# A four-layer attention kernel whose step order, engine choices and buffer assignment are replaced as a whole

## The chip, the cores and the metric

The kernel runs on one core of a Trainium2 chip. The core has five engines that each work through a queue of their own in order: TensorE (PE, matmuls into the eight banks of PSUM), VectorE (DVE), ScalarE (ACT), GpSimd (POOL) and SyncE (SP, which here does nothing but issue DMA transfers). Engines wait for each other through semaphores. The metric is the device time in microseconds from the start of the program to its end, as the median of several runs.

## The reference

A sequence of 2048 rows of 512 values in bf16 goes through four layers: A, B, A, B. Each layer normalises its input, computes attention with 32 heads of 16 values, multiplies with an output matrix and adds the result to its input. Both A layers share one set of weights, both B layers another.

```python
def _A_ref(x, wqkv, w_phi, wo):                    # H = 32, Dh = 16
    ...
    pq = jnp.einsum("bhsd,hdf->bhsf", q, w_phi)
    pk = jnp.einsum("bhsd,hdf->bhsf", k, w_phi)
    phi_q = jnp.concatenate([_softmax(pq, axis=-1), _softmax(-pq, axis=-1)], axis=-1)
    phi_k = jnp.concatenate([_softmax(pk, axis=-1), _softmax(-pk, axis=-1)], axis=-1)
    kv = jnp.einsum("bhsf,bhsd->bhfd", phi_k, v)
    z  = jnp.einsum("bhsf->bhf", phi_k)
    ...
    o = num / den                                   # num = phi_q kv, den = phi_q z + 1e-6
    return o_reshaped @ wo

def _B_ref(x, wqkv, wo):
    W, dil = 8, 2
    ...
    idx = pos[:, None] - off[None, :]               # each row sees itself and 7 rows before, 2 apart
    ...
    attn = _softmax(logits, axis=-1)
    o = jnp.einsum("bhsw,bhswd->bhsd", attn, vg)
    return o_reshaped @ wo

x = x + _A_ref(_layernorm(x), A_wqkv, A_w_phi, A_wo)
x = x + _B_ref(_layernorm(x), B_wqkv, B_wo)
x = x + _A_ref(_layernorm(x), A_wqkv, A_w_phi, A_wo)
x = x + _B_ref(_layernorm(x), B_wqkv, B_wo)
```

## The kernel before

**Tiles.** The 2048 rows are cut into four blocks of 512 columns, called block 0 to 3 below. `x` stays in SBUF from the first layer to the last. Within a block most tiles are 128 x 512: `xn` (normalised `x`), `xnT` (its transpose, on PE through `ident` at L478 to L490, or by a DMA at L473), `K`, `QT`, `V`, `oT` (the attention's result, transposed).

**Layer A.** For each block, `a1` makes the feature maps of the keys: PE multiplies (L616), ACT takes the exponential (`Ek`, L622), DVE sums and divides (L649 to L674), PE multiplies the values (L628) and adds up the key-value sums (L691). The values are copied to `vaug` by ACT or DVE. `a2` does the same for the queries (L721, `Eq` L729), and PE sums each softmax with 32 small matmuls (`ms`, L737). Once the sums over all four blocks are there, `akv` copies them to `kvT`, PE transposes them (L767) and DVE writes them into `ZM` (L776) and `R` (L780). Then come the denominators (`a3`, L805 to L872) and the output (`a4`, L924, L543).

**Layer B, general form.** `b1` makes `K`, `QT` and `V` of a block (L951). K and V carry a few columns of the block before (the halo). SP copies V eight times into `Vg`, once for each place in the window (L1012). `b2`: DVE multiplies `QT` with shifted `K` (`prod`, L1043, 128 x 4096 values in one instruction), PE adds the products up per head through `indQK` (L1050), ACT takes the exponential, and the softmax ends with `PT` (L1078) on DVE. `b3`: DVE multiplies `PT` with `Vg` (`pav`, L1105, 128 x 4096 values), PE adds up through `indAV` (`mo`, L1114, 32 x 32 matmuls with `pav` as the weights), the result is copied to `oT`, and four matmuls with `WoB` (L543) make the output of 128 rows. There are four `pav` and four `mo` per block.

**The last block.** Block 3 of the second B layer has a form of its own (`e1` to `e4`): scores as small matmuls (`sc`, L1278), the exponential `ex` (L1299), a mask on DVE (`msk`, L1304), `mo` as 64 tiny matmuls (L1322), the division by the sums (`ln`, `rd`, L1338 and L1341) as DVE's `oB` (L1349), PE's transposes to `oT`. It goes in four parts `t` = 0 to 3.

**The residual.** For each 128 rows a `res` step adds the layer's output to `x`. It has two forms: DVE adds from PSUM (L556), or PE adds `x` in PSUM through a matmul with `ident` (L546) and ACT copies the sum out (L553). ACT's squares `sqd` (L563) and a few small operations then give the mean and the deviation for the next layer's `xn` (L466 on DVE or L468 on ACT). In the last layer `x` goes to the output (L567) instead.

**What sets the order.** Nothing is scheduled by rule. All work is recorded as 1488 small steps, each a few instructions that belong together, in named threads (`step`, L188). `run` (L1450) plays them in the order that the string `_ORDER` gives, one name in base 36 after the other. Since every engine works in order, this string fixes the queue of every engine, of PE, DVE, ACT, POOL and of SP's DMA issues. A `flex` step (L196) may run on two engines; the string `_CHOICE` holds a bit for each. For copies and `xn`, 1 is DVE and 0 is ACT; for `res`, 1 is the form with PE and ACT; for `bev`, 1 lets DVE read PSUM with no copy by ACT.

**Buffers.** Each tile asks `slot` (L161) for the next entry of `_SLOTS` of its kind: `med` (16 buffers), `ps` (eight PSUM banks), `big` (eight buffers of 128 x 4096, for `prod`, `pav`, `Vg` and others) and `t2` (six). A tile waits for the tile that had its buffer before. So the strings also fix who waits for whom.

**The flag.** The fast form is right only where some sums stay in bounds. The `flag` steps count this: two on DVE, one on PE. Then every engine loads the flag from memory (`flag`, L1411) and branches (`If`, L2069): where the flag is set, `_general_path` computes all again. With this input it isn't set. `_OPT["flag_lag"]` is 12: the load is issued as the twelfth step counted from the last DVE flag step, on SP between the stores of the output.

Of the kernel before, what the change touches and what calls it, by code (L numbers as in the profile page):

```python
# [52 lines left out]
    "flag_lag": 12,  # L53
# [8 lines left out]
8 2e a d c 23 i i i 0 j 9 k j l i 2 i i i i 0 b o p i f 2 0 1m 1m 1o m n i i i i 1n 1m 1m 1p 1q 1m 1r o q r 1m t  # L62
4 z 1s s z i 3 1t 1u 21 z z 10 3 1t i7 1v 22 22 21 1 24 24 2p z 0 t u 13 11 15 1t 1t t 16 1w 1t 1y 12 12 12 12
1x x 1t 5 v w w 25 y 14 2f 2f 18 18 18 18 1z 2g 2c 17 6 19 18 1c 1d 39 2d 1b 1a 2d 22 22 1f 1f g 21 22 22 3a 3a
2c 2c 1f 2d 20 21 1f 22 2c 7 7 20 20 22 26 29 1g 1f 1k 39 3a 2d 2d 2d 2d 1i h 3b 2f 24 2i 1h 1e 29 1j 1l 2q 2h
27 2d 2n 3c 2o 2o 29 29 2a 39 2k 2k 3a 2k 2k 2n 2n 2n 2q 2o 2o 2r 3a 3a 2q 2q 2o 2o 2o 29 2y 2y 2l 2s 2k 2o 2z
2z 2z 2z 31 31 36 3c 33 24 36 36 28 36 2y 2y 2v 2v 2z 2v 37 36 2z 2z 2z 2f 2j 2u 2v 2b 2w 2b 2b 2b 2m 36 2m 36
2m 36 36 2m 39 3a 3b 3b 31 2v 2t 3a 31 32 4e 37 3c 34 35 39 3a 2x 2x 3c 2x 30 2x 38 38 36 38 38 3i 3c 3b 3c 3c
3c 7 3d 3e 3e 3j 3k 3k 3b 3k 3c 3l 5h 3m 3n 3m 3d 3e 3d 3l 5i 3o 3m 3e 3e 3l 3p 3m 3q 3r 3m 3m 5j 3d 3v 5i 3e 3e
3s 3e 20 20 20 20 3t 3m 5h 3u 5n 3m 3m 5m 3d 3e 7c 5h 5q 5o 5p 5r 5k 5i 3f 3g 3g 7 3f 3g 3g 5l 3m 5i 5i 7d 3w 3x  # L70
5i 5i 3z 5i 5i 3f 3f 7e 5i 5s 3g 3y 3g 40 41 7d 5w 42 7f 41 41 7f 41 5t 7f 3g 5v 3g 5u 5x 44 43 45 bd 43 43 46
43 47 5y 3f 43 47 48 90 5x 5x 4b e 49 4c 60 61 41 41 4a 41 41 3g 5x 5z 5z 4d 4g 4g 4h 5z 62 5z 4l 4l 4l 91 92 7d
7d 7g 63 4i 5z 91 4f 4n 4q 4q 4m 4q 63 66 67 64 65 7j 7i 7h 4l 7k 4r 93 4g 4g 4j 4w 4w 7l 7l 4o 4w 7o 68 4k 4q
4u 93 93 4t 4s 4f 7l 7p 7m 7n 4p 4v 7n 7l 7q 6p 6k 6k 4v 6k 7n 7n 91 91 6f 6g 7r 6n 6m 6k 6a 6a 4w 94 6l 7n 69
7r 7u 6o 7v 96 7t 97 4x 95 7s 7w 98 4x 4x 4x 6f 6c 6h 4y 4y 6a 6d 6b 6r 6r 99 6f 6i 6r 99 3h 99 99 9d 9e 3h 6f
6j 6a 6e 9a 9b 9c 9b 6r 9b 9b 83 7y 7y 84 9f 9b 8d 7z 6s 6s 6s 9f 9h 6s 6t 6t 88 89 9i 7y 6s 6t 4w 4x 83 83 6q
6q 7y 6q 85 88 4y 88 8b 83 9g 87 86 81 b2 9j 9k 88 8c 9m 9n 8f 9w 9x 82 9w 9w a1 6r 9z 69 6u 9w 80 6u 6v 8a 6u
6v 6x 6v 4w 6w 6q 6u 6v 6y 9m 4v 4z 4z 6z 4v 70 71 4z 4z 70 70 9y 72 7x 73 72 74 70 75 72 72 76 9o 9r 9r 50 51
8f 50 50 72 52 76 78 8e 8e 50 53 77 54 9r 9u 79 7a 9m 9p 7b 8f 9s 9t 55 8e 56 57 8f 55 58 55 55 59 8g 8g 8g 8e
a0 8g 57 57 a3 9r 5a 57 9v 9m 9q 5b a3 57 5b 8h 8h 5c b3 5e 5d 5f 5g 7x 9l a2 b0 b0 a3 b1 b1 b1 8g 8h b1 b3 b3  # L80
b6 b3 b7 bz c0 c0 a4 a4 a4 a3 a4 a5 a5 bz c0 c0 bz d3 b4 bz c0 c0 c0 c0 8f 8i b0 b1 a4 8i 8i 8i a5 as at b0 b1
# [12 lines left out]
ex ey ey f8 fa dm dm dm dm ew f0 fa f6 f2 hu hv f5 es ga dn dn hw f1 dk i1 i2 i1 dl dm f9 f9 i3 c6 i6 i6 i6 hx
hw hw dn hy fb i6 fa fb fa fb hz fb fc hu gl fc fb c5 fc gl dl do gn gl c6 dp do dp i1 i1 fa i6 i6 gb i8 i4 i9
gc i9 i5 ib go ia i6 f9 f9 i9 i9 i6 do ie id gb i6 i6 i6 dr gm gg gh hw i0 gd gg gi ic ic dp ds dq do dp dt ic
fd fe fd fe fd fg fe i6 i6 i6 i6 fh i6 c5 gb ge ic ff ic gg gj if ic ic if ic ic ic if ig ig gq gg gb gl gk gf
ig gs gs gs if if ig ig gp du if ig gs gt gt gt gt if gu ig if du du gu du dv ic c5 ic ic fd ih fe ih ih dy ig
ih ic dz ic dw ii ii fi ij gr gr gt ij ik ij ij fj fj ik il ga gu il in gs fl ii ij ij gv ii fj fj im ij ij ik
il ik fn fo gr gr il gw gx iq io iq iq gv gw gv gw gv gv ip iq iv dx dx fk fm fm gy gz h2 is gw gw ir it h2 iw  # L100
iu h0 it ix iw h3 h3 h4 h5 h6 h2 h1 h3 h7 h2 h5 h3 h8 h5 h5
# [4 lines left out]
    "0010110111100111111111000000100000100110011100000111011110010100000101010000100000000000111101011100"  # L106
    "1010010100001100100000000000000011111110000100001010100000000000000000010111001000001101000000000000"
    "1010000011111100000000000100010110011011010100101111000000001001000000010110010001000100011100100000"
    "00000000011111010000011100000000000000000000000001000011001000000000000000001100"
)  # L110


_SLOTS = {
    "med": (
        "0123456789abcdef346aff72ffc3105f92b4de6a7fd92b317ef99962c0517dbf2e3abf6925cd13e273a31dad901d74235cdb"
        "f72a94d35c017b9264acf31d08"
    ),
    "ps": (
        "0123124350123021456715604156734153267234701623047237452365001230210345672135304675261473045672350146"
        "1401230453013042567103651251741023452036714302310345031240230435406703203501467012012457245201240310"  # L120
        "3245602750235102563740130473024567142362047540123640760437034563745101021345067241301456701236204531"
        "7024560124567326452016435735601247351204561203460750264012312301203405367136731421432102324567467556"
# [15 lines left out]
class _Fast:  # L138
# [1311 lines left out]
    def run(self):  # L1450
        self.setup()
        self.stages()
        n, left = {}, None
# [647 lines left out]
```

## Time and profile before

| | us |
|---|---|
| median of 3 runs | 329.32 |
| the three runs | 329.32, 327.63, 330.07 |
| span of the profiled execution | 327.7 |
| DVE `pav` L1105, 29 instructions | 63.3, one 2.219 |
| DVE `prod` L1043, 28 instructions | 62.9, one 2.285 |
| PE projections of B L951, 336 matmuls | 76.7, one 0.380 |
| ACT exponentials L622 and L729, 64 each | 33.9 and 34.7 |

The time of the profiled execution is its span, 327.7 us, 1.6 below the median. The page lists each engine's busy time over that span; PEld are PE's weight loads, which run beside its matmuls. In rows of groups, `A<-B` means that the instruction writes tile A from tile B, `x45` counts instructions, and the numbers behind the bar are the busy time of all, the mean ns of one, and the idle time of the engine just ahead of them, with the tile that ended the wait. In rows of the timeline the first number is when the group starts in the span, the second how long it lasts, and a bracket holds the idle time ahead of it. In rows of stretches come the stretch, its length, the busy time of PE, PEld, DVE, ACT and POOL (each with its count of instructions), the share of full speed at which PE's clock was granted, the busy share of the DMA engines and the GB/s.

The layers follow each other and overlap: the last `mo` of the first A (L924) starts at 98.2 us, when the first projections of B (from 77.3 us) are long under way; the last `mo` of the first B (L1114) starts at 177.3, the first keys of the second A (L616) at 148.0; the second A's last `mo` starts at 242.1 us, and the tiny matmuls of the last block (L1322) run from 298.3 to 308.9.

### The profile page before, as it was taken

The page shows a single profiled execution, that of the slowest core. Times are in us where ns is not written, and L with a number is a line of the kernel's source. Part 1 is how long each engine was busy: PE and PEld are TensorE (multiplying, and loading weights), DVE is VectorE, ACT ScalarE, POOL GpSimd, SP SyncE. Part 2 cuts the span into 40 slices and gives each one's busy share as a digit, 9 for nine tenths or more (in the row PEclk, how much of TensorE's full clock was granted, in tenths as well). Part 3 has the DMA queues.
Part 4 walks back from the last instruction along what each step waited for, and adds up shares of the span by engine and source line. Part 5 has one row for each costly group of instructions (what it writes and reads, how often), then busy time and mean ns, then how long its engine had stood idle before and what let it go on. Part 6 is the DMA issues. An engine that isn't in the chain of part 4 may idle for free.

```text
span 327.7 us, 8877 instructions
## 1 busy us (share of the span) xinstructions
PE 308.8 (94%) x3542; PEld 153.5 (47%) x3574; DVE 296.3 (90%) x456; ACT 278.1 (85%) x640; POOL 39.1 (12%) x64
## 2 busy tenths in 40 slices
PE   7999999899999999999999999789999999986993
PEld 3644456444444454444444455543545444443441
DVE  6899995989999999999999999599898999999493
ACT  4999989999789977999999999799898866987360
POOL 6000000000020006000000000000040395210000
PEclk9999999999999999999999999999999999999799
DMA  7964300023677979679991200050588997549814
GB/s 203 341 162 90 108 2 4 2 68 81 144 172 140 132 149 158 108 131 131 145 121 28 40 0 4 4 141 9 145 147 121 192 136 131 135 83 176 158 67 137
DMA packets 45793, 36.41 MB, mean 111 GB/s; under 512 B 30832, under 2 KB 41136, under 8 KB 45744
## 3 DMA queue, kind: packets, MB, share of 16 engines
q1 hardware_dynamic: 45216, 35.75, 56.2%
q8 instruction: 30, 0.49, 0.7%
q14 instruction: 19, 0.16, 0.2%
q10 hardware_dynamic: 528, 0.02, 0.1%
HBM read 11.13 MB, written 3.25 MB: 44 GB/s over the span
## 4 chain that ended last, share of the span: by engine, by line
DVE 31%; ACT 31%; PE 18%; issue 12%; DMA 3%; SPq 2%; DVEq 0%; ACTq 0%
DVE prod L1043 6%; ACT Eq L729 5%; DVE pav L1105 5%; PE PS L543 5%; ACT sqd L563 5%; ACT Ek L622 4%; DVE x L556 4%; DVE Ek L674 3%; PE PS L951 3%; DVE xn L466 3%; ACT oT L205 2%; PE PS L1050 2%; DVE s L649 2%; ACT xn L468 2%; DMA wraw<-in_A_wqkv_dram 1%
## 5 line engine op out<-in xcount | busy, mean ns | idle before, releaser
L951 PE MATMUL PS<-xnT,WB 128*128 128x512 bf16 x336 | 76.7, 380 | 0.3 <-ACT K L205 0.2
L1105 DVE TENSOR_TENSOR pav<-PT,Vg 128x4096 bf16<-128x4096 bf16 (+1 forms) x29 | 63.3, 2219 | 0.6
L1043 DVE TENSOR_TENSOR prod<-QT,K 128x4096 bf16<-128x4096 bf16 x28 | 62.9, 2285 | 0.4 <-ACT QT L205 0.3
L951 PEld LDWEIGHTS <-WB 128*128 128x128 bf16 x336 | 37.3, 114 | 37.1 <-issue 4.2
L543 PEld LDWEIGHTS <-oT 128*128 128x128 bf16 x240 | 22.5, 98 | 31.3 <-issue 5.6
L729 ACT ACTIVATE Eq<-PS 128x512 bf16<-128x512 f32 x64 | 34.7, 624 | 0.0
L622 ACT ACTIVATE Ek<-PS 128x512 bf16<-128x512 f32 x64 | 33.9, 627 | 0.0
L563 ACT ACTIVATE sqd<-x 128x512 bf16<-128x512 bf16 x48 | 30.4, 633 | 2.1 <-DVE x L556 1.2
L721 PE MATMUL PS<-xnT,WA 128*128 128x512 bf16 x128 | 31.1, 380 | 0.2 <-ACT bs L870 0.2
L543 PE MATMUL PS<-WoB,oT 128*128 128x512 bf16 x105 | 27.7, 393 | 3.1 <-issue 2.9
L616 PE MATMUL PS<-WA,xnT 128*128 128x512 bf16 x124 | 29.9, 379 | 0.5 <-DVE x L556 0.2
L628 PE MATMUL PS<-WA,xnT 128*128 128x512 bf16 x122 | 29.9, 379 | 0.3
L543 PE MATMUL PS<-WoA,oT 128*128 128x512 bf16 x119 | 29.3, 380 | 0.8 <-DVE x L556 0.2
L556 DVE SCALAR_TENSOR_TENSOR x<-PS,x 128x512 bf16<-128x512 f32 x45 | 28.9, 684 | 0.3 <-PE PS L543 0.2
L205 ACT CAST oT<-PS 128x512 bf16<-128x512 f32 (+1 forms) x47 | 24.8, 595 | 3.8 <-PE PS L1114 3.5
L616 PEld LDWEIGHTS <-xnT 128*128 128x128 bf16 x128 | 12.3, 98 | 15.0 <-issue 0.6
L628 PEld LDWEIGHTS <-xnT 128*128 128x128 bf16 x128 | 12.3, 98 | 14.4
L205 ACT CAST V<-PS 128x512 bf16<-128x512 f32 x27 | 15.4, 591 | 4.1 <-PE PS L951 4.1
L674 DVE TENSOR_TENSOR Ek<-Ek,rk 128x4096 bf16<-128x4096 bf16 (+1 forms) x10 | 18.6, 1860 | 0.3 <-ACT rk L669 0.3
L721 PEld LDWEIGHTS <-WA 128*128 128x128 bf16 x128 | 11.7, 97 | 15.2 <-issue 2.0
L205 ACT CAST K<-PS 128x512 bf16<-128x512 f32 x30 | 17.4, 591 | 0.3 <-PE PS L951 0.3
L466 DVE TENSOR_SCALAR xn<-x,rstd,nmr 128x512 bf16<-128x512 bf16 x46 | 16.8, 408 | 0.6
(164 smaller groups left out, 496.9 us busy)
## 6 DMA issues: line engine op xcount, KB each, us to landing
Vg<-V SPq DMA_DIRECT2D x112, 131.5 KB, 4.8
Prho<-rd SPq DMA_DIRECT2D x8, 512.0 KB, 5.4
x<-in_A_x_dram SPq DMA_DIRECT2D x3, 512.0 KB, 5.8
WB<-in_B_wqkv_dram SPq DMA_DIRECT2D x3, 512.0 KB, 8.6
out_dram<-x SPq DMA_DIRECT2D x6, 256.0 KB, 2.3
wraw<-in_A_wqkv_dram SPq DMA_DIRECT2D x4, 256.0 KB, 5.4
vd<-Vs SPq DMA_DIRECT2D x2, 272.0 KB, 3.3
x<-in_A_x_dram SPq DMA_DIRECT2D x4, 128.0 KB, 3.9
```

Source lines behind the costliest of these rows:

```text
L205: self.nc.scalar.copy(out=out, in_=in_)
L543: nc.tensor.matmul(y[:], lhsT=lh(t, c), rhs=Wo()[:, c, :], start=(c == 0), stop=(c == NB - 1 and not onpe))
L556: nc.vector.scalar_tensor_tensor(out=xb[:, t, :], in0=T[t][:], scalar=1.0, in1=xb[:, t, :], op0=ALU.mult, op1=ALU.add, **kw)
L563: nc.scalar.activation(out=sqd[:], in_=xb[:, t, :], func=ACT.Square, accum_out=T["ss"][:, t:t + 1])
L616: nc.tensor.matmul(pk[:], lhsT=xnT[:, t, k, :], rhs=self.WA[:, k, D:2 * D], start=(k == 0), stop=(k == NB - 1))
L622: nc.scalar.activation(out=T["E"][:, t, s, :], in_=T["k", t][:], func=ACT.Exp, scale=1.0 - 2.0 * s)
L628: nc.tensor.matmul(pv[:], lhsT=xnT[:, t, k, :], rhs=self.WA[:, k, 2 * D:3 * D], start=(k == 0), stop=(k == NB - 1))
L721: nc.tensor.matmul(pq[:], lhsT=self.WA[:, k, hb * P:(hb + 1) * P], rhs=xnT[:, :, k, :], start=(k == 0), stop=(k == NB - 1))
L729: nc.scalar.activation(out=self.Eq[L, b][s][:, :, hb, :], in_=T[hb][:].rearrange("p (t i) -> p t i", t=4), func=ACT.Exp, scale=1.0 - 2.0 * s)
L951: nc.tensor.matmul(pp[:], lhsT=self.WB[:, k, i * D + c:(i + 1) * D:NB], rhs=xnT[:, :, k, :], start=(k == 0), stop=(k == NB - 1))
L1043: nc.vector.tensor_tensor(out=pr[:], in0=QT[:, c:c + 1, :].to_broadcast([P, NW, TB]), in1=win, op=ALU.mult)
L1105: nc.vector.tensor_tensor(out=pv, in0=PT[:, :, lo:lo + n].unsqueeze(1).to_broadcast([P, NB, 2, n]), in1=vw, op=ALU.mult)
```

## The change

The diff replaces `_ORDER`, `_CHOICE` and four of the five strings of `_SLOTS`; the fifth, `pp`, stays. None of the functions that issue instructions is changed. The flag's load becomes a step of its own (`read`), placed by `_ORDER` like any other, and here it is the last step of all. `flag_lag` goes.

```diff
-    "flag_lag": 12,
...
 _ORDER = """
-8 2e a d c 23 i i i 0 j 9 k j l i 2 i i i i 0 b o p i f 2 0 1m 1m 1o m n i i i i 1n 1m 1m 1p 1q 1m 1r o q r 1m t
...
-iu h0 it ix iw h3 h3 h4 h5 h6 h2 h1 h3 h7 h2 h5 h3 h8 h5 h5
+ce e4 4f 8 i i i i i i i i i 23 5k ck i i f a 3t 3u d 2 9 0 h e 3r 5o 5l ci e3 3p 0 1m 3o i j o 2 ch k b j l 4
...
+gw h0 gw h2 iv h3 h1 h3 h2 h3 h2 iw iu it it h4 h5 h6 h7 h3 h5 h5 h8 h5 iy
 """
...
 _CHOICE = (
-    "0010110111100111111111000000100000100110011100000111011110010100000101010000100000000000111101011100"
...
+    "1010111111110111111110100000100000011000000000000111011110000100001101010110000000000000110111101100"
...
     "big": (
-        "012345670123456012345617234561720351724361720436170425361725362503421034210354276"
+        "472307531426351062154643273172617351305205426165704562316152365205402314240230610"
...
+        def read():
+            self.redo = self.flag()
+
         add("flag", "DVE", counts)
         add("flag", "PE", total)
         add("flag", "DVE", decide)
+        add("flag", "ALL", read)
...
-        n, left = {}, None
+        n = {}
         for w in _ORDER.split():
             key = self.names[int(w, 36)]
             i = n.get(key, 0)
             n[key] = i + 1
             self.threads[key][i]()
-            if key == "flag.DVE" and i == 1:
-                left = _OPT["flag_lag"]
-            if left is not None:
-                left -= 1
-                if left == 0:
-                    self.redo = self.flag()
-        if left is None or left > 0:
-            self.redo = self.flag()
```

Decoded, the new strings do this to the instructions. The counts of all instructions that run on one engine alone stay the same. Of the steps that may run on two engines, 5 copies of `vaug`, 4 of `oT` and one of half `kvT` go from DVE to ACT; 3 `xn` and one `xnT` go from ACT to DVE; 3 `res` go from PE with ACT to DVE, so that the matmuls with `ident` fall from 19 to 16. At the start, SP issues the half key weights first and the weights of B in one go behind `x`, and eleven instead of nine warm-up matmuls stand ahead of PE's first transposes. At both turns from keys to queries the transposes of `kvT` come earlier in PE's queue: four query matmuls stand ahead of them instead of eight in the first A, and all of a block's `ms` behind them instead of ahead in the second. In the second B, block 0's four `mo` come late and in a row, and block 1's third `pav` takes the buffer that its first `pav` had. In the last block, the first two `mo` stay side by side, and the third and fourth do as well; 18 output matmuls, three `res`, one mask and two `pav` stand between the first two parts' `oB` and the third's. The code above the flag moves up by one line, so that every line number below `flag_lag` is one less in the changed kernel, up to the flag steps.

More of the change, by code (lines that the diff above doesn't have):

```diff
@@ L67 @@
[L67 to L81, printed above, removed]
@@ new lines @@
+3 3 1m m 0 0 i p o 2e 1 q 6 1n 1o z i r 5 1m 1m z n z 1m z s 20 20 20 20 1t 20 1m 1p 1t 1v 1q 1r 1s 21 20 7 21
+1u 10 24 z 22 1t 11 22 13 t 1t 1t 15 12 25 1x 16 12 22 14 24 t 18 e7 22 1t 1w 18 12 12 1z 2c 17 u t v x 2d 2d
+2c 2c 2c 2f 18 2d w 26 w 2d 18 2f 2d 2p 1f 2d y 19 1y 18 1b 1c 1a 1d 2f 1e 2g 20 2d 1f 39 2i 2h 1f 39 3a 7 1f
+21 2d 39 3a 3a 2k 3a 1g 1f 5q 1j 2f 21 7 7 3a 1i 24 24 1h 22 22 c 22 2n 22 2j 1k 2n 3a 27 29 29 1l 2n 2o 2n 2k
+2o 3s 2o 29 29 2o 28 2o 2q 3b 2o 2o 2o 2v 2a 2y 2z 2z 2y 2y 2k 2z 29 2z 2y 2z 2z 31 2k 2r 2l 31 36 2v 2q 36 36
@@ new lines @@
+2q 2z 2z 33 3c 39 36 2b 2b 2k 2v 32 2t 37 2b 2b 2m 2m 2v 3a 2m 3b 36 36 g 2q 3c 2w 31 3a 3c 2s 2v 31 36 36 36
+35 34 39 30 3c 2m 2x 37 2x 2x 2u 3b 3c 36 3a 3b 2x 38 38 38 38 3d 3c 3i 3j 3c 3k 3c 3e 3b 3k 3l 3m 5h 3e 3d 3c
+3n 3e 3e 3d 3k 3m 3l 5i 3e 3m 3l 3m 3q 3m 3d 3e 5j 3m 5i 3v 3e 3e 5h 3m 5i 3d 5m 3m 7c 5i 5n 3m 3e 7d 3m 5h 5i
+5i 5p 5i 5i 5i 5r 3f 3g 3g 3f 3g 3w 3g 3f 3x 3z 5i cd 3y 7e 40 3f 3g 3g 7d 7f 5s 7f 5u 3g 41 5t 3g 41 5v 7f 41
+42 5w 43 44 41 45 43 46 5x 43 43 5y 5x 47 3f 43 90 3g 60 47 48 49 5x 4c 41 4b 91 41 41 41 4d 5x 4a 92 4q 91 93
@@ L110 @@
+    "1000000011111100000000000000100110011011100100111010100011000100000000001110010000010010011010000000"
+    "00000000011010101000011100000000000000000000000000000001000000000000000000001000"
 )
```

73 lines of the change are left out of this document (38 added, 35 removed).

## The prediction

> **What bounds the kernel now.** I read the page's busy times first, then the chain of waits, then the stretches of the span, then groups of instructions for prices, and last the timeline where the change moves something.
>
> ```profile
> PE 308.8 (94%) x3542; PEld 153.5 (47%) x3574; DVE 296.3 (90%) x456; ACT 278.1 (85%) x640; POOL 39.1 (12%) x64
> ...
> DVE 31%; ACT 31%; PE 18%; issue 12%; DMA 3%; SPq 2%; DVEq 0%; ACTq 0%
> ```
> ```profile
> 0.00:53.00 53.00, 50.42 (x555) 27.55 (x561) 46.85 (x102) 45.85 (x97) 6.09 (x35) 1.00 0.52 140
> 53.00:207.00 154.00, 150.71 (x1569) 73.50 (x1581) 145.43 (x205) 144.59 (x336) 10.26 (x16) 1.00 0.54 93
> 207.00:327.70 120.70, 107.70 (x1420) 52.46 (x1432) 104.03 (x149) 87.67 (x210) 22.74 (x13) 0.98 0.63 121
> ```
> ```profile
> 280.00:300.00 20.00, 18.73 (x400) 9.34 (x401) 19.44 (x14) 17.28 (x43) 3.51 (x2) 1.00 0.59 125
> 300.00:310.00 10.00, 7.33 (x175) 3.90 (x176) 5.21 (x6) 4.07 (x13) 0.00 (x0) 0.83 0.97 180
> ```
>
> Three engines are nearly full (columns of the stretches: PE, PEld, DVE, ACT, POOL). From 53 to 207 us each has at most 9.4 us without work, so the chain jumps between them and no single one sets the time. Only after 207 us is there slack: 13.0 us on PE and 16.7 us on DVE, and 4.8 us of DVE's lie between 300 and 310. A new order can win there, or win by doing less work on whichever engine the chain runs through. It has as much room to lose: two or three engines at 94% cover nothing.
>
> The profiled execution took 327.7 us; the median of the runs is 329.32. I make the sum on 327.7 and add 1.6 at the end.
>
> **Term 1: work that changes its engine.** The `_CHOICE` bits move these steps. DVE loses 5 copies of `vaug`, 4 of `oT` and one of half `kvT`, and gains 3 `xn`, one `xnT` of 1024 columns and 3 residual adds `x`. ACT takes and gives the counterparts. PE loses 3 matmuls with `ident` (the residual added in PSUM).
>
> ```profile
> L466 DVE TENSOR_SCALAR xn<-x,rstd,nmr 128x512 bf16<-128x512 bf16 x46 | 16.8, 408 | 0.6
> L556 DVE SCALAR_TENSOR_TENSOR x<-PS,x 128x512 bf16<-128x512 f32 x45 | 28.9, 684 | 0.3 <-PE PS L543 0.2
> L203 DVE CAST oT<-PS 128x512 bf16<-128x512 f32 x14 | 9.4, 682 | 0.0
> L203 DVE CAST vaug<-PS 128x512 bf16<-128x512 f32 x8 | 5.4, 679 | 0.0
> L205 ACT CAST oT<-PS 128x512 bf16<-128x512 f32 (+1 forms) x47 | 24.8, 595 | 3.8 <-PE PS L1114 3.5 <-PE PS L924 0.2
> L205 ACT CAST vaug<-PS 128x512 bf16<-128x512 f32 x24 | 13.4, 604 | 0.0
> L468 ACT ACTIVATE xn<-x,nmr,rstd 128x512 bf16<-128x512 bf16 x18 | 14.3, 814 | 1.7 <-DVE nmr L457 1.7
> L553 ACT ACTIVATE x<-PS 128x512 bf16<-128x512 f32 x19 | 11.2, 598 | 2.0 <-PE PS L546 2.0
> L205 ACT COPY xnT<-PS 128x1024 bf16<-128x1024 bf16 (+1 forms) x6 | 5.3, 891 | 0.0
> L546 PE MATMUL PS<-x,ident 128*128 128x512 bf16 x19 | 7.7, 406 | 0.0
> ```
>
> DVE: 3 x 0.408 + 3 x 0.684 + 0.68 - 5 x 0.679 - 4 x 0.682 - 0.5 = -2.7 us (the `xnT` copy is put at an `oT` cast's 0.68, of as many bytes; the half `kvT` costs at most one, 0.68 on DVE and 0.60 on ACT, and I take 0.5 for it on both). ACT: 4 x 0.595 + 5 x 0.604 + 0.5 - 3 x 0.814 - 3 x 0.598 - 0.89 = +0.8 us. PE: -3 x 0.406 = -1.2 us. Everything else is the same count of the same instructions. Weighted with the engines' shares of the chain: -2.7 x 0.31 + 0.8 x 0.31 - 1.2 x 0.18 = **-0.8 us**. The ends are -2.7 (all of DVE's saving lies on the path) and +0.8 (ACT's extra lies on it and nothing is won).
>
> **Term 2: the two turns from keys to queries.** When the last sums of `kvT` are done, PE transposes it and DVE makes `ZM` from it; both wait in a row.
>
> ```profile
> 52.01 1.90 PE L721 MATMUL PS<-xnT,WA 128*128 128x512 bf16 x8
> 52.12 0.69 DVE L203 CAST kvT<-PS 128x512 bf16<-128x512 f32 x1 [0.96 <-PE PS L691]
> 53.75 0.39 PE L767 MATMUL PS<-ident,kvT 128*128 128x128 bf16 x4
> ...
> 54.27 0.29 DVE L776 TENSOR_TENSOR ZM<-PS,maskH 128x32 bf16<-128x32 bf16 x2 [1.46 <-PE PS L767]
> ```
> ```profile
> 206.53 0.58 ACT L205 CAST kvT<-PS 128x512 bf16<-128x512 f32 x1
> 207.19 0.52 PE L737 MATMUL PS<-Eq,indS 128*32 128x128 bf16 x24 [0.48 <-ACT kvT L205]
> 207.64 0.40 PE L767 MATMUL PS<-ident,kvT 128*128 128x128 bf16 x4
> ...
> 208.15 0.29 DVE L776 TENSOR_TENSOR ZM<-PS,maskH 128x32 bf16<-128x32 bf16 x2 [2.15 <-ACT rS L743]
> ```
>
> In the first turn `kvT` is ready at 52.81 and PE comes to it at 53.75, because eight query matmuls stand ahead; after the change four do, so up to 0.9 us goes. In the second it is ready at 207.11 and the transposes start at 207.64, behind 24 of the 32 small matmuls of `ms`; the change puts `ms` behind them: up to 0.5 us. What is late next is the same in both: the denominators' chain between ACT and DVE. I take half of it, **-0.7 us** (0 to -1.4), since the PE work put behind the transposes delays the next softmax sums.
>
> **Term 3: the last 30 us.** Here DVE carries the end, with one large hole.
>
> ```profile
> 298.45 0.83 DVE L1304 TENSOR_TENSOR et<-et,maskW 128x1280 bf16<-128x1280 bf16 x1 [0.22 <-ACT et L1299]
> ...
> 300.39 1.28 DVE L1349 TENSOR_TENSOR oB<-PS,rdB 128x512 bf16<-128x512 f32 x2
> ...
> 302.03 0.69 DVE L1078 TENSOR_TENSOR PT<-E,rden 128x1024 bf16<-128x1024 bf16 x1 [0.35 <-ACT rden L1073]
> 302.62 1.43 PE L543 MATMUL PS<-WoB,oT 128*128 128x512 bf16 x4 [2.55 <-issue]
> ...
> 304.27 1.91 PE L543 MATMUL PS<-WoB,oT 128*128 128x512 bf16 x4
> ...
> 309.45 0.69 DVE L1349 TENSOR_TENSOR oB<-PS,rdB 128x512 bf16<-128x512 f32 x1 [4.41 <-ACT rdB L1341]
> ...
> 310.10 1.03 PE L543 MATMUL PS<-WoB,oT 128*128 128x512 bf16 x4
> ```
> ```profile
> q8 instruction: 30, 0.49, 0.7%
> ```
>
> After two `mo` steps of block 3 of the second B (64 tiny matmuls and as many weight loads each) PE stands 2.55 us on nothing that the profile shows. Then four matmuls take 1.43 and four 1.91 us, against 1.03 later: 0.4 + 0.9, and some 0.5 for two `ident` matmuls between, make 1.8. So the stop costs PE 2.55 + 1.8 = 4.4 us. I read it as a wait for instructions: 30 packets in 0.49 MB are 16 KB each, and nothing in the kernel runs through instructions as fast as these steps. DVE, in order, stands 4.41 us at the third `oB`, since between the second and the third it has only `PT` and one `pav` (0.69 + 2.28 us, the price of a `pav` by the row under term 4).
>
> [...]
>
> The new order keeps those two `mo` steps side by side, so I keep the stop. It gives DVE more to do between the second and third `oB`: three residual adds, `PT`, one mask and two `pav`, 3 x 0.684 + 0.69 + 0.83 + 2 x 2.28 = 8.1 us for 3.0. But PE has more there too, 18 output matmuls that were done earlier before, at 0.217 us each (eight in 1.90, four in 1.03): 3.9 us. From the end of the two `mo` steps (302.62 - 2.55 = 300.07) to the third `oB` it took 9.4 us, and will take 13.3; DVE, whose second `oB` ends 1.6 us after them, comes to it at 1.6 + 8.1 = 9.7. The hole shrinks from 4.8 (4.41, and 0.35 ahead of `PT`) to 3.6: **-1.2 us**. Without the stop `oB` is ready at 8.9, DVE never waits, and 4.8 go. With a second stop at the third and fourth `mo`, which stand side by side as well, the hole is 8.0: +3.2.
>
> The flag's load goes from ahead of the last steps to behind them.
>
> ```profile
> L2069 SPq EVENT_SEMAPHORE  x8: 17/17/17, 324.6 to 326.3; - x8
> ...
> L2069 PEldq COMPARE_BRANCH  x1: 3606/3606/3606, 321.4 to 321.4; - x1
> ```
>
> The dearest branch, PE's, runs from 321.4 to 325.0. Behind PE's last matmul it would start about 0.9 us later and end at 325.9, still before SP has seen the last store land at 326.3: 0, and at most +1 if that cover of 0.4 us is gone. It also takes SP's load out from between the stores, which wait for DVE anyhow.
>
> **Term 4: waits that the new order brings.** Eight `big` buffers hold the products of DVE until PE has summed them, and the replicated V (`Vg`).
>
> ```profile
> 282.33 2.37 PE L1114 MATMUL PS<-pav,indAV 128*32 128x512 bf16 x40
> ```
> ```profile
> 272.65 11.38 DVE L1105 TENSOR_TENSOR pav<-PT,Vg 128x4096 bf16<-128x4096 bf16 x5
> ...
> 283.94 6.69 DVE L1043 TENSOR_TENSOR prod<-QT,K 128x4096 bf16<-128x4096 bf16 x3
> ```
> ```profile
> Vg<-V SPq DMA_DIRECT2D x112, 131.5 KB, 4.8
> ```
> ```profile
> 272.31 4.97 SPq L1012 DMA_DIRECT2D Vg<-V  x8
> ```
>
> In the second B the new order sums block 0's four `pav` late and at once, and block 1's third `pav` takes the buffer of its first. From block 0's last `pav` DVE gets there after `PT`, two `pav` and two `prod`: 0.69 + 2 x 2.28 + 2 x 2.23 = 9.7 us. PE must by then have done the sum of that `pav`, nine projection steps of four matmuls (0.87 each) and the sum of block 1's first. The two sums are 16 packed matmuls; at 0.06 us, PE's pitch where a row above shows 40 of them in 2.37 us, that makes 1.0 + 7.8 = 8.8. The margin is 0.9 us. The `Vg` rows for that same `pav` are issued behind block 0's second sum, which comes about 1.2 us ahead of the last `pav`'s end: 4 x 0.62 to issue and 4.8 to land make -1.2 + 2.5 + 4.8 = 6.1 of 9.7 us. Behind this `pav` DVE has the next `prod` and the mask steps, for which ACT and PE wait. I take **+0.5 us**, with 0 and +4.4 (DVE's longest wait in the trace) as ends.
>
> **The first 53 us.** SP issues the same loads in another order: the first half of the key weights leads, the loads of B's weights follow in one go behind `x`, and eleven instead of nine warm-up matmuls stand ahead of the first transposes. The bytes ahead of `WA`'s third part grow by 128 of some 2,400 KB. I cost it at 0: PE can win at most its 2.6 us without work there, and I let it lose as much.
>
> Sum: -0.8 - 0.7 - 1.2 + 0.5 = -2.2; 327.7 - 2.2 = 325.5, and 1.6 for the median: **327.1 us**.
>
> **Rivals.** The forecast (0.30): as summed; for it speaks that all large costs stay where they were. The order does not matter (0.08): the three full engines set the time whatever stands first; 329.3; the 3 to 9 us that each engine has free from 53 to 207 us speak for it, the open 16.7 us after 207 against it. Faster (0.32): the stop after the `mo` steps does not come back, since block borders in PE's instructions fall elsewhere; term 3 is -4.8, span 321.9, median 323.5. [...] Against it: the two steps are as dense as before. Slower (0.30): PE gives buffers back late. The place is block 1's third `pav`, the margin 0.9 us; every us of PE beyond that is a us at the end, as DVE has 0.6 us of slack from 280 to 300. A stop as above costs PE 4.4 us, and 2.7 more of shorter waits for evictions make 7.1: 6.2 us on DVE in place of the 0.5, and 325.5 + 5.7 + 1.6 = 332.8. It becomes a loss of over 1% from 6.7 us on. For it: PE had 1.3 us to spare in those 20 us, and dense steps (eight score steps) lie there as well.
>
> **How the numbers follow.** A measurement of this kernel tells about 1% from no change (the three runs spread over 0.7%). The likeliest is 327.1, 0.7% below before. The distances of each part's ends from the value taken, squared, added and rooted: below, 1.9, 0.7, 3.6, 0.5 and 2.6 make 4.9, so 322; above, 1.6, 0.7, 4.4, 3.9 and 2.6 make 6.7, so 334. Both rivals lie inside. All ends at once are unlikely, so I draw it in to 322.5 and 333.0, with some 2 in 10 outside. Faster than 326.0: 0.32. Within: 0.38, from the forecast and the rival of no change. Slower than 332.6: 0.30.
>
> **What would show it.** Term 1: DVE's busy time near 293.6, ACT's near 279, PE's near 307.6. Term 2: `ZM` starts within 1.2 us of the `kvT` copy's end. Term 3: the wait ahead of the third `oB` under 4 us, and whether PE stands over 2 us after two `mo` steps. Term 4: DVE's idle time ahead of L1104 (L1105 before) under 1 us from 250 to 300. The prediction is wrong if a wait over 3 us stands ahead of a `pav` or `prod`, or if the first 53 us, which I cost at nothing, change by over 1.5 us.

## The result and the profile after

| | us |
|---|---|
| before, median of 4 runs | 329.26 (327.63 to 330.07) |
| changed, median of 4 runs | 324.77 (324.14 to 324.93) |
| ratio, with its 95% interval | 0.9858 [0.9828, 0.9888] |
| span of the changed kernel's profiled execution | 323.2 |

The changed kernel is 1.4% faster. The forecast was 327.1, or 0.7%: the direction was right, the gain twice as large, and the time came out between the forecast and the rival called faster (323.5).

First the page of the changed kernel: busy times, and the chain of waits by engine. Line numbers are one lower than before.

```profile
PE 308.5 (95%) x3571; PEld 152.2 (47%) x3571; DVE 293.4 (91%) x454; ACT 276.2 (85%) x642; POOL 41.5 (13%) x64
...
PE 79%; ACT 7%; DMA 5%; SPq 3%; issue 2%; DVE 1%; ACTq 0%; DVEq 0%
...
L1104 DVE TENSOR_TENSOR pav<-PT,Vg 128x4096 bf16<-128x4096 bf16 (+1 forms) x29 | 63.0, 2214 | 0.3
```

DVE has 2.9 us less to do. The chain jumped between engines before and now runs through PE for 79% of the span; of the 12% of "issue", time in which an engine waited for nothing shown, 2% are left. DVE waits 0.3 us in all ahead of the `pav`.

Then the stretches of the changed kernel, in the columns PE, PEld, DVE, ACT, POOL, PE's clock, DMA share, GB/s.

```profile
0.00:53.00 53.00, 51.53 (x562) 27.37 (x563) 44.96 (x102) 46.61 (x100) 5.67 (x34) 1.00 0.52 140
53.00:207.00 154.00, 151.83 (x1643) 73.77 (x1642) 144.96 (x209) 143.38 (x335) 16.24 (x17) 1.00 0.55 93
207.00:323.20 116.20, 105.19 (x1370) 51.09 (x1368) 103.45 (x145) 86.19 (x208) 19.61 (x13) 0.99 0.60 125
280.00:300.00 20.00, 18.70 (x386) 8.84 (x385) 19.02 (x17) 16.54 (x44) 3.69 (x2) 1.00 0.60 136
300.00:310.00 10.00, 10.00 (x240) 5.89 (x239) 9.97 (x14) 6.64 (x16) 0.00 (x0) 1.00 0.64 188
```

The last row stands against that of before: from 300 to 310 us PE was busy for 7.33 us at a clock of 0.83, and DVE for 5.21; now both are full and the clock is 1.00.

The timeline of PE around the first two `mo` steps of the last block (they lie between the first row and the second), and that of DVE behind them:

```profile
292.83 1.05 PE L1049 MATMUL PS<-prod,indQK 128*32 128x512 bf16 x16
...
295.04 1.04 PE L542 MATMUL PS<-WoB,oT 128*128 128x512 bf16 x4
295.92 0.59 PE L1065 MATMUL PS<-E,indDen 128*128 128x512 bf16 x2
```
```profile
295.71 1.28 DVE L1348 TENSOR_TENSOR oB<-PS,rdB 128x512 bf16<-128x512 f32 x2
...
304.45 1.27 DVE L1348 TENSOR_TENSOR oB<-PS,rdB 128x512 bf16<-128x512 f32 x2
...
313.92 1.89 DVE L555 SCALAR_TENSOR_TENSOR x<-PS,x 128x512 bf16<-128x512 f32 x3 [1.01 <-PE PS L542]
316.28 0.69 DVE L555 SCALAR_TENSOR_TENSOR x<-PS,x 128x512 bf16<-128x512 f32 x1 [0.48 <-PE PS L542]
```

PE goes from the second `mo` to the output matmuls with no bracket, that is with no idle time of note: the stop of 2.55 us is gone, and four of those matmuls take 1.04 us instead of 1.43 and 1.91. The third `oB` on DVE has no wait; before it was 4.41 us. The wait that is gone is about as long as the measured gain of 4.5 us. Work has moved across this place too, so the two timelines alone don't prove that the gain comes from there. The question for the runs was whether the order took the stop away, or something else.

### The profile page after: what moved, and what is told of

It is laid out like the page before. It is cut to its first block, busy times and chain, and to the rows that moved or that the text cites. A ratio compares the mean times of both kernels' runs of the same rounds, so it can differ in the third digit from the quotient of the medians.

```text
span 323.2 us, 8879 instructions
## 1 busy us (share of the span) xinstructions
PE 308.5 (95%) x3571; PEld 152.2 (47%) x3571; DVE 293.4 (91%) x454; ACT 276.2 (85%) x642; POOL 41.5 (13%) x64
## 4 chain that ended last, share of the span: by engine, by line
PE 79%; ACT 7%; DMA 5%; SPq 3%; issue 2%; DVE 1%; ACTq 0%; DVEq 0%
PE PS L950 20%; PE PS L542 15%; PE PS L615 9%; PE PS L627 9%; PE PS L720 6%; PE PS L1049 4%; PE PS L1113 3%; ACT Eq L728 3%; PE PS L690 2%; DMA Prho<-rd 2%; DMA wraw<-in_A_wqkv_dram 1%; ACT bs L869 1%; PE PS L481 1%; SPq L1011 1%; PE PS L1185 1%
## 5 line engine op out<-in xcount | busy, mean ns | idle before, releaser
L1042 DVE TENSOR_TENSOR prod<-QT,K 128x4096 bf16<-128x4096 bf16 x28 | 63.8, 2284 | 0.9 <-PE PS L1049 0.4
L728 ACT ACTIVATE Eq<-PS 128x512 bf16<-128x512 f32 x64 | 35.5, 613 | 0.6 <-PE PS L720 0.6
L555 DVE SCALAR_TENSOR_TENSOR x<-PS,x 128x512 bf16<-128x512 f32 x48 | 31.7, 683 | 2.2 <-PE PS L542 2.0
L720 PE MATMUL PS<-xnT,WA 128*128 128x512 bf16 x128 | 31.9, 380 | 0.2 <-DVE Eq L838 0.2
L204 ACT CAST oT<-PS 128x512 bf16<-128x512 f32 (+1 forms) x51 | 28.4, 598 | 4.0 <-PE PS L1113 3.0
L627 PE MATMUL PS<-WA,xnT 128*128 128x512 bf16 x128 | 31.0, 379 | 0.0
L615 PE MATMUL PS<-WA,xnT 128*128 128x512 bf16 x128 | 30.6, 379 | 0.0
L542 PE MATMUL PS<-WoA,oT 128*128 128x512 bf16 x128 | 30.2, 380 | 0.0
L542 PE MATMUL PS<-WoB,oT 128*128 128x512 bf16 x112 | 27.0, 379 | 0.0
L465 DVE TENSOR_SCALAR xn<-x,rstd,nmr 128x512 bf16<-128x512 bf16 x49 | 18.3, 416 | 0.5
L204 ACT CAST vaug<-PS 128x512 bf16<-128x512 f32 x29 | 17.2, 612 | 0.6 <-PE PS L627 0.6
```

What stands on the lines that cost most here:

```text
L204: self.nc.scalar.copy(out=out, in_=in_)
L542: nc.tensor.matmul(y[:], lhsT=lh(t, c), rhs=Wo()[:, c, :], start=(c == 0), stop=(c == NB - 1 and not onpe))
L555: nc.vector.scalar_tensor_tensor(out=xb[:, t, :], in0=T[t][:], scalar=1.0, in1=xb[:, t, :], op0=ALU.mult, op1=ALU.add, **kw)
L615: nc.tensor.matmul(pk[:], lhsT=xnT[:, t, k, :], rhs=self.WA[:, k, D:2 * D], start=(k == 0), stop=(k == NB - 1))
L627: nc.tensor.matmul(pv[:], lhsT=xnT[:, t, k, :], rhs=self.WA[:, k, 2 * D:3 * D], start=(k == 0), stop=(k == NB - 1))
L720: nc.tensor.matmul(pq[:], lhsT=self.WA[:, k, hb * P:(hb + 1) * P], rhs=xnT[:, :, k, :], start=(k == 0), stop=(k == NB - 1))
```

## The experiments: what makes the stop

PE's stop showed as "issue", and the prediction read it as a wait for instructions. If that is so, it should depend on where the two dense `mo` steps lie in PE's list of instructions. A place below is a number in that list as compiled, weight loads, matmuls and PE's few waits counted alike; the recorded instructions were matched to it in order, which fixes a border to about two places. The trace records PE's instruction packets, 30 of 16 KB each; from one to the next it is about 256 places in the mean: in the changed kernel 5390 recorded instructions of PE lie between the packet at 61.74 us and the one at 305.15, 21 distances on, 257 for each. The two `mo` are 256 instructions; the 250 behind their last wait fill 6339 to 6588 in the kernel before and 6301 to 6550 in the changed one.

The test moves all later instructions by a known number of places and touches neither order nor engines nor buffers: some warm-up matmuls at the start are cut into narrower ones of about the same total width. The diff shows the case of nine for one, in the first eight warm-ups (64 more matmuls); four for one in the first seven give 21 more, three for one in the first thirteen 26.

```diff
         def warm():
             if not hasattr(self, "warm_ps"):
                 self.warm_ps = self.ps()
+            self.nwarm = getattr(self, "nwarm", 0) + 1
+            if self.nwarm <= 8:
+                for _ in range(9):
+                    nc.tensor.matmul(self.warm_ps[:, 0:56], lhsT=self.kvT[:, 0:P], rhs=self.kvT[:, 0:56],
+                                     start=True, stop=True)
+                return
             nc.tensor.matmul(self.warm_ps[:], lhsT=self.kvT[:, 0:P], rhs=self.kvT[:], start=True, stop=True)
```

The kernel before with 64 more matmuls, the changed kernel with 21, and the changed kernel with 64:

> The kernel before, with 64 more PE matmuls in its warm-up: each of the first eight warm-up matmuls of 512 columns becomes nine of 56 columns. Nothing else changes, so every later PE instruction moves up by 128 places. Block theory: PE gets its instructions in blocks of 256 and asks for a block when it enters the one ahead of it; in the kernel before, the two dense mo steps fill places 6339 to 6588, almost exactly one block (6336 to 6591), so that PE runs through it before the next one is there. Moved by 128, a border falls into the middle of the dense steps: the stop of 2.55 us and the slow matmuls behind it go, the third oB waits under 1 us instead of 4.41, and the time falls by 3 to 4.8 us less at most 1 for the longer warm-up: 325 to 327. Rival, that the stop belongs to these steps or to the transfers that run beside them: it stays over 2 us, 329 to 330.

> The changed kernel, with 21 more PE matmuls in its warm-up: each of the first seven warm-up matmuls of 512 columns becomes four of 128. Every later PE instruction moves up by 42 places, and the first two dense mo steps, at 6301 to 6550 in the changed kernel, come to 6343 to 6592, the place that they had in the kernel before. Block theory: the stop comes back, over 2 us behind the second mo, with slow matmuls behind it, and the time rises by 2 to 4.4 us: 327 to 329. Rival, that the new order or the work beside it took the stop away: no stop, 324.5 to 325.5.

> The changed kernel, with the same 64 more warm-up matmuls as the first run of this set. The dense steps come to 6429 to 6678 and 6787 to 7042, with a block border in the middle of each or close to its end. Block theory: no stop, 324.5 to 326, the excess being what the longer warm-up costs. Rival: the same. It shows what the added matmuls cost by themselves.

| kernel | us, median | ratio to before | stop of PE behind place |
|---|---|---|---|
| before | 329.6 | 1 | 2.55 us, 6592 |
| before, 64 more | 328.16 | 0.997 [0.9943, 0.9996] | 0.97 us, 7104 |
| changed, 21 more | 327.64 | 0.9942 [0.9911, 0.9972] | 2.36 us, 6592 |
| changed, 64 more | 326.62 | 0.993 [0.9902, 0.9958] | 2.08 us, 7104 |

These are the rows of PE's timeline at the stops: first the changed kernel with 21 more, then with 64 more, then the kernel before with 64 more.

```profile
292.49 1.04 PE L1055 MATMUL PS<-prod,indQK 128*32 128x512 bf16 x16
...
297.29 1.02 PE L548 MATMUL PS<-WoB,oT 128*128 128x512 bf16 x4 [2.36 <-issue]
```
```profile
304.58 0.67 PE L1371 MATMUL PS<-ident,oB 128*32 128x128 bf16 x15
307.33 0.28 PE L1371 MATMUL PS<-ident,oB 128*32 128x128 bf16 x1 [2.08 <-issue]
```
```profile
301.35 0.61 PE L1072 MATMUL PS<-E,indDen 128*128 128x512 bf16 x2
...
308.83 0.60 PE L1372 MATMUL PS<-ident,oB 128*32 128x128 bf16 x12
310.39 0.84 PE L1372 MATMUL PS<-ident,oB 128*32 128x128 bf16 x20 [0.97 <-issue]
```

The stop comes back in the changed kernel as soon as its dense steps lie at 6343 to 6592. The added matmuls themselves cost nothing there: L1055 starts at 292.49, L1049 without them at 292.83. With 64 the stop at 6592 is gone from both orders, and a new one stands where I had not expected any: between place 7104 and 7106, within rows of like transposes. I had counted the matmuls between dense step and border as wide ones; they are these transposes. 6592 and 7104 lie 2 x 256 apart, so the new stop is at a border of the same grid. In the changed kernel it stands ahead of the last of 16 transposes, in the kernel before ahead of the 13th of 32: nothing but the place sets them apart from their neighbours. The kernel before gained only 1.4 us: it came to the dense steps late (L1072 at 301.35 where L1066 was at 299.69) and had the second stop.

When PE entered a block, when the next packet came, and when PE went on, from the matched trace:

| kernel | border | block before it entered | packet | PE goes on |
|---|---|---|---|---|
| before | 6592 | 298.34 | 299.68 to 301.16 | 302.62 |
| changed, 21 more | 6592 | 293.37 | 295.10 to 296.03 | 297.29 |
| changed, 64 more | 7104 | 302.87 | 304.79 to 305.82 | 307.33 |
| before, 64 more | 7104 | 305.26 | 307.45 to 308.93 | 310.39 |
| changed | 6592 | 293.87 | 295.14 to 296.59 | no stop: reached at 298.30 |

In these rows a packet starts 1.3 to 2.2 us after the block ahead of it is entered, so I take it as asked for about then. PE goes on 1.3 to 1.5 us after it has landed, 3.9 to 5.1 us after that entry. In the kernel before the two `mo` run through a whole block in 1.3 us. In the changed kernel the border at 6336 falls 35 places into them, and the 42 places from their end to 6592 are output matmuls, sums of `pav` and three others, which take 3.3 us: PE came to the border 1.7 us after the packet had landed, so just in time.

With these times I looked for the shift at which the kernel before runs through no block too fast: 52 places.

> The kernel before, with 26 more PE matmuls in its warm-up: each of the first thirteen warm-up matmuls of 512 columns becomes three of 170. Later instructions move up by 52 places: the dense mo steps come to 6391 to 6640 and 6729 to 6984, and no block of 256 (borders at 6336, 6592, 6848, 7104) is run through in under 4 us. Block theory: neither the stop of 2.55 us nor a new one of over 0.5 us; the time falls by 2.5 to 4.5 us, to 325 to 327, more than with 64 matmuls, which left a stop of 0.97 us at place 7104 and put PE back by 1.7 us on the way there. Rival, that what PE wins in the last part is lost again whatever the place: 328 to 329.5, as with 64.

| kernel | us, median | ratio to before |
|---|---|---|
| before, 26 more warm-up matmuls | 324.38 (323.4 to 326.75) | 0.987 [0.9833, 0.9908] |

PE's and DVE's timelines of that run, at the places of the stop and of the hole:

```profile
299.29 0.60 PE L1072 MATMUL PS<-E,indDen 128*128 128x512 bf16 x2
299.74 1.03 PE L549 MATMUL PS<-WoB,oT 128*128 128x512 bf16 x4
```
```profile
300.02 1.28 DVE L1355 TENSOR_TENSOR oB<-PS,rdB 128x512 bf16<-128x512 f32 x2
...
304.89 0.69 DVE L1355 TENSOR_TENSOR oB<-PS,rdB 128x512 bf16<-128x512 f32 x1 [0.23 <-ACT rdB L1347]
```

Up to the second `oB` this run is that of before to 0.4 us (300.02 against 300.39). Behind it the third `oB` waits 0.23 us instead of 4.41, and starts at 304.89 instead of 309.45. The old order with 26 more narrow matmuls is as fast as the change: 0.987 against 0.9858, with intervals of 0.3 to 0.4% to either side. So PE's stops cost the kernel before some 4.3 us, nearly all of it at 6592, and the new order is worth 0.4 us where neither has them, which can't be told from nothing. Where both stop at 6592 the new order wins 0.6% (changed, 21 more). DVE's rows of that run fit the reading that it has more work to do meanwhile; its waits between the second and the third `oB` add up to 2.3 us instead of 4.76:

```profile
298.35 1.29 DVE L561 SCALAR_TENSOR_TENSOR x<-PS,x 128x512 bf16<-128x512 f32 x2 [1.68 <-PE PS L548]
300.26 0.69 DVE L1083 TENSOR_TENSOR PT<-E,rden 128x1024 bf16<-128x1024 bf16 x1 [0.62 <-ACT rden L1078]
...
306.61 1.28 DVE L1354 TENSOR_TENSOR oB<-PS,rdB 128x512 bf16<-128x512 f32 x2
```

## The experiments: engines, the flag, the turn

**Engines.** The strings `_CHOICE` of the two kernels differ in 65 of 380 bits. They were exchanged, then only the 17 bits of `xn`, then only the 27 of the copies in the A layers.

The first of four lines, here of the kernel before with the change's bits:

```diff
 _CHOICE = (
-    "0010110111100111111111000000100000100110011100000111011110010100000101010000100000000000111101011100"
+    "1010111111110111111110100000100000011000000000000111011110000100001101010110000000000000110111101100"
...
```

> The kernel before, with the changed kernel's engine choices alone; order and buffers stay. The first term of the prediction: -0.8 us, between -2.7 and +0.8, so about 328.5. The dense steps stay at 6337 to 6586 and the stop stays. If engine choices made most of the measured gain of 4.5 us, it is 325 to 326.5; if choices fit only the order that they were searched with, it is slower than before, 330 or more.

> The changed kernel, with the engine choices of the kernel before; order and buffers stay those of the change. By the first term of the prediction it loses 0.8 us, between -0.8 and +2.7: about 325.6. If most of the gain is the choices', 328 or more. The dense steps lie at 6303 to 6552, so no stop is expected.

> The changed kernel, with the kernel before's engine for the 17 xn steps that the change moved: by count DVE loses 3 xn (-1.2 us) and ACT gains 3 (+2.4 us). Pricing by count, as in the prediction's first term: +0.4 us, 325.2. Theory that a choice is right only for its place in the order: several us of the 19 that all 65 choices cost together, 327 or more.

> The changed kernel, with the kernel before's engine for the 27 copies in the A layers (vaug, oT, xnT and the first layer's) that the change moved. By count DVE gains 4.8 us and ACT loses 3.9: +0.3 us weighted, +4.8 if all of DVE lies on the path: 325 to 329.6. Theory that a choice is right only for its place: beyond DVE's 4.8 us, 330 or more.

| kernel | us, median | ratio to before |
|---|---|---|
| before, the change's engines | 355.26 | 1.0831 [1.0786, 1.0877] |
| changed, the engines of before | 345.09 | 1.0446 [1.0407, 1.0486] |
| changed, 17 `xn` as before | 329.50 | 1.0011 [0.9991, 1.0032] |
| changed, 27 copies in A as before | 331.99 | 1.0072 [1.004, 1.0104] |

The page of the kernel before with the change's engines, its busy times, and the first of DVE's and of PE's waits (in total, how often, the longest):

```profile
PE 314.8 (89%) x3571; PEld 153.6 (44%) x3571; DVE 295.1 (84%) x454; ACT 279.7 (79%) x642; POOL 43.2 (12%) x64
```
```profile
DVE q L575 <- ACT sqd L563: 6.5, 7, 3.5
DVE QT L203 <- PE PS L951: 5.0, 1, 5.0
```
```profile
PE PS L951 <- DVE x L556: 5.4, 2, 3.3
```

DVE has 1.2 us less to do than in the kernel before and the run takes 26 us longer: the engines wait for each other in more places and for longer (of the three rows only the first was there before, with 4.3 us and 1.1 as the longest). PE's stops are a small part of it: the stop at 6592 stays, with 2.1 us, and one of 1.7 us stands at the next border. The other way round it is 19 us. Seventeen `xn` whose net effect by count was 0.4 us cost 4.7; 27 copies priced at 0.3, or at 4.8 with all of DVE's share on the path, cost 7.2; in neither of these two runs does PE stop at a border. In these four runs a choice of engine was good only together with the order and the other choices that it came with, and what it removed from an engine in sum did not tell its price.

**The flag.** `flag_lag` raised to 1000 in the kernel before, so that the load comes last; in the changed kernel the step `read` moved ahead of the last three stores.

> The kernel before, with the flag's load behind all other steps, as in the changed kernel. The prediction costs this at 0, at most +1: 329.3 to 330.3. If the late load delays the last store, as a store landing of 4.1 us in the changed kernel against 2.7 before might have it, +1 to +1.5.

> The changed kernel, with the flag's load issued ahead of the last three stores, where the kernel before had it. By the prediction no difference: 324.3 to 325.3. If the late load is what makes the last store land late, the last 1 to 1.5 us come back: 323.3 to 323.8.

Measured: 329.28 us, ratio 0.9998 [0.9976, 1.002], and 325.07 us, 0.9866 [0.9834, 0.9898] against 0.9858 of the change itself. The flag's place costs nothing in either order, as predicted. That the changed kernel needed 6.2 us from the end of DVE's last `x` (316.97) to the end of its span, and the kernel before 4.7 (its last `x` ends at 322.96), isn't the flag's doing: with the flag early it was 5.5. Over all profiled executions the old order needed 4.2 to 5.1 us for this stretch, the new one 5.5 to 6.7 in eight of nine and 4.2 in one. So the new order seems to lose about 1 us between its last `x` and the end; what sets it was not tried.

**The turn.** In the changed kernel ZM starts 0.57 us after the end of the copy `kvT` in both turns. The timeline, first and second turn:

```profile
52.61 0.69 DVE L202 CAST kvT<-PS 128x512 bf16<-128x512 f32 x1 [1.25 <-PE PS L690]
...
53.87 0.29 DVE L775 TENSOR_TENSOR ZM<-PS,maskH 128x32 bf16<-128x32 bf16 x2 [0.57 <-PE PS L766]
```
```profile
204.51 0.58 ACT L204 CAST kvT<-PS 128x512 bf16<-128x512 f32 x1
...
205.66 0.29 DVE L775 TENSOR_TENSOR ZM<-PS,maskH 128x32 bf16<-128x32 bf16 x2 [2.15 <-PE PS L766]
```

To see what that is worth, the second turn was undone, and a little more: PE's steps `ms` of block 2 and the first four query matmuls of block 3 went ahead of the transposes.

```diff
 kv kv kv kv (block 3)
+ms (block 2)
 akv ev
+rs (block 2), mq 0 (block 3)
 akv tr, z, z
-ms (block 2)
 akv r
-rs (block 2)
 md, dr (block 0)
-mq 0 (block 3)
```

> The changed kernel; in the second A's turn, block 2's 32 ms matmuls and block 3's first four query matmuls are put ahead of the four transposes of kvT again (rS on ACT behind the copy of kvT), each tile keeping its buffer. That is more than the order of before had there: 0.7 + 0.87 us of PE work ahead of ZM. Second term of the prediction: what stands ahead of the transposes is on the path at a half, +0.5 to +1.6 us: 325.5 to 326.5. Rival, that PE's queue is full anyway and only the order within it changes: under 0.3 us, 324.6 to 325.1.

Measured: 324.26 us, ratio 0.9868 [0.9835, 0.9901], no different from the change. The timeline of PE tells where the delay went; first the changed kernel, then the run with the turn undone (where the same matmul has L1259):

```profile
205.15 0.40 PE L766 MATMUL PS<-ident,kvT 128*128 128x128 bf16 x4 [0.68 <-ACT kvT L204]
...
284.02 0.26 PE L1277 MATMUL PS<-Qbd,K 64*32 64x160 bf16 x5
285.22 0.29 PE L1277 MATMUL PS<-Qbd,K 64*32 64x160 bf16 x9 [0.94 <-DMA Qbd<-Qs]
```
```profile
205.74 0.39 PE L748 MATMUL PS<-ident,kvT 128*128 128x128 bf16 x4
...
284.57 0.26 PE L1259 MATMUL PS<-Qbd,K 64*32 64x160 bf16 x5
285.14 0.28 PE L1259 MATMUL PS<-Qbd,K 64*32 64x160 bf16 x9 [0.31 <-DMA Qbd<-Qs]
```

The transposes are 0.59 us late, PE is 0.55 us late for 80 us on end, and then the wait for the transfer of `Qbd` shrinks from 0.94 to 0.31 us and both go on together (285.22 and 285.14). In the changed kernel, whatever PE wins ahead of that transfer, up to 0.94 us, it gives back there. That suggests a version of its own: bring the transfer forward. Three of the loads of `Qbd` stand in SP's queue behind loads of the last block's values that nobody needs yet.

```diff
 vrep 2 (block 1)
+qsc 5, qsc 6, qsc 7 (second half)
 vrd 0, vrd 1, vrd 2
-qsc 5 (second half)
 vrd 3, pav 0 (block 1)
-qsc 6, qsc 7 (second half)
```

> The changed kernel; on SP's queue the last three of the sixteen loads of Qbd, for which PE stands 0.94 us at 284.02, go ahead of the four loads of the last block's values (vd) that stand between them, and are issued from about 279.1 to 281 us instead of 281.1 to 283.7. PE's own order does not change. If PE carries the time here, the wait goes and the kernel gains up to 0.9 us: about 324 us, and at places beyond 285 us the same instruction starts 0.9 us sooner. Rival, that ACT's exponentials and DVE's masks behind the first scores are as late as before: the wait goes, and what follows at 289 us starts where it did; 324.5 to 325.

Measured: 323.38 us (322.52 to 324.3), ratio 0.9806 [0.9763, 0.9849]. The timelines of PE and of DVE in this run:

```profile
284.03 0.33 PE L1259 MATMUL PS<-Qbd,K 64*32 64x160 bf16 x16
```
```profile
294.87 1.28 DVE L1330 TENSOR_TENSOR oB<-PS,rdB 128x512 bf16<-128x512 f32 x2
```

The wait for `Qbd` is gone, and the first two `oB` start at 294.87 where the change has 295.71. This is the fastest kernel of the study, 1.4 us under the change by medians and 1.5 by profiled spans (321.7 against 323.2); the intervals of the two ratios overlap a little, while the earlier start of 0.8 us is plain in the trace.

## Why the prediction was right and wrong

**The step that failed** is the sentence in the third term, "The new order keeps those two `mo` steps side by side, so I keep the stop." The stop was read rightly as one of instructions, and the rival called faster named the right condition: that borders in PE's instructions fall elsewhere. But I weighed the likelihood by how dense the steps are, which did not change, and not by their place, which decides. The compiled program of both kernels was there to count: 250 places of dense steps against a grid of 256. In the kernel before they fill one block almost exactly; in the changed one a border falls 35 places into them, and the stop is gone. With the stop put back (changed, 21 more) the time is 0.9942 of before, 327.4 us; the forecast for that case was 327.1. That agreement is in part luck: DVE's hole was 2.3 us there where the sum had 3.6, PE's matmuls behind the stop weren't slowed (1.02 us for four), and terms 1 and 2 did not hold as they were summed.

**Term 1**, engines. The busy times came as worked out for DVE (293.4 for 293.6), not for ACT: 276.2, where it should have risen from 278.1 to 279. PE's can't be compared, since the trace of before lacks 32 of its 3574 matmuls. The price of -0.8 us could not be found back: exchanging the choices alone moves the time by 19 to 26 us, so their share of the change can't be measured apart from the order.

**Term 2**, the turns. `ZM` does start within 0.57 us of the copy's end. But undoing the second turn cost nothing that could be measured: what it wins ends at the wait for `Qbd`. A wait for `Qbd`, of 1.0 us, was in the trace of before, and the prediction didn't ask what stands between a turn at 207 us and the end. The first turn was not undone by itself. The reading of the second turn was wrong as well. The 24 `ms` matmuls that stood ahead of the transposes (the prediction's row at 207.19) did not wait for the copy `kvT`, which they don't read: PE stood at a border, place 4288. With 26 more matmuls in the old order the border lies elsewhere, and all 32 run in a row while the copy is still under way (it ends at 207.29):

```profile
206.60 0.63 PE L743 MATMUL PS<-Eq,indS 128*32 128x128 bf16 x32
207.35 0.40 PE L773 MATMUL PS<-ident,kvT 128*128 128x128 bf16 x4
```

There `ZM` starts at 207.85, as close behind the copy as in the new order. So the new order won at this turn, too, what another place of the border wins.

**Term 3**, the tail. Without the stop I gave 4.8 us for the new order; in the old order, taking PE's stops away was worth 4.3 (26 more matmuls: 0.987). That the flag costs nothing was right.

**Term 4**, late buffers. I took +0.5 with a margin of 0.9 us at block 1's third `pav`. DVE waits 0.3 us in all for its 29 `pav`, so the margin held, and the rival called slower did not come about. No run narrowed that margin.

**The first 53 us** were costed at 0; ZM starts at 53.87 for 54.27. Right.

Taken together, the terms other than the stop were forecast at -1.0 and came to about -0.4 +/- 1.6 (the change against before with 26 more): too small to be told from none.

## What to carry to other kernels

A stop of PE that no semaphore explains, in or right behind a dense row of small matmuls, can be one of place, as the 2.55 us at 6592 were: count the row's instructions, weight loads too, and where they begin against blocks of 256, the distance of the packets in these traces. The profile may put such a stop down to another engine, as it put 0.48 us at 4288 down to ACT's `kvT`; whether the matmul reads that tile tells. It can be moved with a few narrow matmuls where PE has time (26 in the warm-up took the 2.55 us away, 21 brought 2.36 back), and before a search by timing is believed, its result should be measured with such a shift, or the search may have found the offset and not the order. Before a gain early in the span is counted, look for the next wait on a transfer: here the wait for `Qbd` took 0.94 us with the gain and 0.31 without it, and moving that transfer forward took the wait away and brought DVE's first two `oB` 0.8 us sooner.

## What the runs showed of the hardware

PE's instructions came in packets of 16 KB (30 in 0.49 MB), one per about 256 places (257 recorded instructions, the mean of 21 distances), and one block ahead: at the borders of the table a packet started 1.3 to 2.2 us after the block ahead of its own was entered. Blocks that were run through in about 1.3, 2.1 and 3.9 us cost stops of 2.4 to 2.6, 2.1 and 1.0 us.

The time from entering a block to running the next was 3.9 to 5.1 us at the stops of the table, which all lie in the busy last part of the span. At the border 4288 of the kernel before it was 2.65 us: the block was run through from 204.54 to 206.49 us, the packet came from 204.79 to 205.73, and PE went on at 207.19, again 1.46 us after it had landed. The trace counts 0.48 us of idle time there. The stretches around it and around the stop at 6592:

```profile
204.00:207.00 3.00, 2.71 (x139) 2.10 (x138) 1.99 (x3) 3.00 (x7) 0.00 (x0) 1.00 0.02 5
299.00:303.00 4.00, 1.45 (x73) 1.04 (x62) 3.61 (x7) 2.64 (x10) 0.00 (x0) 1.00 1.04 168
```

The DMA engines moved 5 GB/s at the first and 168 at the second. The packet started 0.25 us after the block ahead of it was entered at the first, and 1.3 us at the second. That full DMA engines delay the packets is my reading; no run took the transfers away.

Behind the stop of 2.55 us the clock was granted at 0.83 from 300 to 310 us. Behind that of 2.36 us in the changed kernel with 21 more it stayed at 1.00, as these stretches of that run show, and the four output matmuls took 1.02 us:

```profile
290.00:300.00 10.00, 7.20 (x201) 3.72 (x200) 7.59 (x8) 6.18 (x20) 0.00 (x0) 1.00 0.61 161
300.00:310.00 10.00, 10.00 (x219) 5.57 (x220) 9.74 (x8) 6.78 (x18) 0.00 (x0) 1.00 0.68 191
```
